# Two padding tiles made longer, so that the large tiles share one address remainder modulo 512

## Chip, cores and metric

The kernel runs on one core of one Trainium2 chip. The metric is the device time of one execution in microseconds (us); of several executions the median counts. The five engines of the core appear under their names in the profile: PE is TensorE (matrix multiply, PEld its loads of the stationary operand), DVE is VectorE, ACT is ScalarE, POOL is GpSimd and SP is SyncE, which only issues transfers here.

## What is computed

A delta-rule attention over 768 steps, then a mixture of 8 experts with Sinkhorn-normalised gates, then a gated two-matrix product with two further projections, all in float32:

```python
def _attn_ref(q, k, v, beta):            # B, H, S, D = 4, 8, 768, 48
    k_n = k / (norm(k) + 1e-6); state = zeros(B, H, D, D)
    for t in range(S):
        y[:, :, t] = einsum('bhd,bhde->bhe', q[:, :, t], state)
        v_old = einsum('bhde,bhd->bhe', state, k_n[:, :, t])
        state += beta[:, :, t] * einsum('bhd,bhe->bhde', k_n[:, :, t], v[:, :, t] - v_old)

def _moe_ref(x, w_gate, w1, w2):         # x (3072, 384), 8 experts, hidden 1024
    P = exp(x @ w_gate - max)
    for _ in range(8):
        P /= P.sum(1); P /= P.sum(0); P *= N / E
    return sum(P[:, e:e+1] * (relu(x @ w1[e]) @ w2[e]) for e in range(8))

def _moe2_ref(x, w1, w2, w3, w_out):     # (384,1024) (384,1024) (1024,1024) (1024,384)
    return (((x @ w1) * (x @ w2)) @ w3) @ w_out
```

## The kernel before

Every float32 operand of the two large products is held as two parts in the type float32r: a rounded value and the rest. A product of two operands is then three matmuls, high by high, high by low and low by high, summed in one PSUM bank. A matmul call names the output, the stationary operand (called the weights here, 128 columns, 512 bytes in each partition) and the moving operand (up to 512 columns, 2048 bytes in each partition). In the rows, `b<-hB,wA` is a matmul into a PSUM bank from operands in the tiles hB and wA; the two names stand in alphabetical order, so that they do not tell which one moves.

There are three stages.

- **Stage A** (to about 425 us): attention in 12 chunks (`prep_k`, `invert`, `tt_make`, `prep_q`, `seq`), and between them the first expert (`e0`) for the chunks that are done, with moving operands of 256 columns from xr and hA and weights from wA. The Sinkhorn loop closes the stage.
- **Stage B** (about 430 to 1745 us): experts 1 to 7. The tokens are taken in three passes of 1024, an expert in two halves, so there are 3 x 7 x 2 = 42 calls of `unit`. A unit first forms `relu(x @ w1)` from linear combinations of blocks (`product`, lines 1222 to 1228: 22 products of three matmuls, moving operands from xr and xT, weights from wA and wS), then multiplies by w2 (`m2`, lines 1270 to 1277: six groups of 12 matmuls, moving operands from hA and hB, weights from wA). All 138 matmuls of a unit have 512 columns. In the first pass the weights come from DRAM through rawB and are split on ACT and POOL; later passes load the split form (`load_pair`).
- **Stage C** (from about 1745 us): the last products, by `phase_c`. w3 and w_out are multiplied first (`m34`: moving operand wA, weights wS, 384 columns, 192 matmuls). Then come six chunks of 512 tokens. In each, 144 matmuls `ab` of 512 columns have their weights in xT and their moving operand, the tokens, in turn in wS and in xr; the 96 matmuls `om` of 384 columns have their weights in hA or hB and their moving operand in wA.

The three matmuls of one product, here in `m2`, where `hv` lies in hA or hB and `wh`, `wl` in wA:

```python
self.mm(o, wh, hv[:, 0], start=(x == 0), stop=False)
self.mm(o, wl, hv[:, 0], start=False, stop=False)
self.mm(o, wh, hv[:, 1], start=False, stop=(x == 3))
```

The order of instructions on each engine is set when the program is built, by a list scheduler (`Plan.order`) that works with cost estimates and knows nothing of addresses. The memory on the chip (SBUF, 128 partitions) is laid out by pools that `open` stacks from the left, in the order of opening, and from the right. A tile has the same address in every partition, rounded up to 32 bytes. Three tiles are never read or written, `padl`, `padr` and `padq`: they only take room and so shift what is stacked after them. `setup` opens the pools of stage A; when the preparation is done, the pool `prep` on the right is closed and rawB, sums, wS and acc are opened in its place, and later `seq` and `xst` on the left give way to xT, and hB, cv, cvr, rt, pb and tmp go to the right.

Of the kernel before, what the change touches and what calls it, by code (L numbers as in the profile page):

```python
# [7 lines left out]
F32 = mybir.dt.float32  # L8
F32R = mybir.dt.float32r
F16 = mybir.dt.float16  # L10
# [12 lines left out]
NE = 8  # L23
# [9 lines left out]
NP = 2  # L33
# [347 lines left out]
class Kernel:  # L381
# [56 lines left out]
    def setup(self):  # L438
# [2 lines left out]
        self.open("const", "left", ones=((128, 128), F32), masks=((128, 148), F32),  # L441
                  wgr=((128, 3, NE), F32), p=((128, NTT + 1, NE + 1), F32),
                  rs=((128, NTT), F32), cs=((128, NE), F32), sml=((128, 8), F32))
        self.open("wg", "left", wg=((128, 3, 2 * NE), F32R), padl=((128, 48), F32))
        self.open("wA", "left", wA=((128, EB, 1536), F32R))
        self.open("hA", "left", hA=((128, HA, 1024), F32R))
        self.open("xr", "left", xr=((128, 2, 2, 2, 3, 128), F32R))
# [7 lines left out]
        self.open("edge", "right", padr=((128, 24), F32))  # L455
        self.open("prep", "right",
                  g12=((128, NG12, 2, NG, 32), F32), a0=((128, NA0, 32, 32), F32),
                  asys=((128, 1056), F32), t=((128, 1056), F32), prod=((128, NP, 1024), F32), xs=((128, 256), F32), bq=((128, 6, 32), F32), t16=((128, 272), F32), padq=((128, 16), F32), wz=((128, 384), F16),
                  wraw=((128, 768), F32))
        self.open("dram", "left", space=DRAM, xs_d=((NCH, 2, DM, 128), F32), y0_d=((3, 128, NT), F32), p_d=((NE, NT), F32), xf_d=((4, 128, 3, 512), F32),  # L460
                  w1_d=((2, 128, 3, 1024), F32), w2_d=((2, 128, 3, 1024), F32), wo_d=((2, 128, 8, DM), F32),
# [1222 lines left out]
```

## Time and profile before

| | us |
|---|---|
| three runs, median (lowest, highest) | 2099.24 (2098.55, 2101.47) |
| the profiled execution, its own time | 2098.41 |
| its span, first to last instruction | 2096.6 |

| engine | busy us | share of the span |
|---|---|---|
| PE | 2066.3 | 99% |
| PEld | 1753.0 | 84% |
| DVE | 1227.3 | 59% |
| POOL | 794.7 | 38% |
| ACT | 729.6 | 35% |

Matmuls are pipelined: one that is recorded with 390 ns overlaps the next, and the time that a matmul takes from a row of matmuls is the distance from its start to the next start. So a PE that is busy all the time may still run through its matmuls faster or slower. That distance is not a column of the profile. It is read from the timeline, where a row gives the start of a merged group and the number of its matmuls: the start of the next group less its own start, over that number.

### The profile page before, as it was taken

The page shows a single profiled execution, that of the slowest core. Times are in us where ns is not written, and L with a number is a line of the kernel's source. Part 1 is how long each engine was busy: PE and PEld are TensorE (multiplying, and loading weights), DVE is VectorE, ACT ScalarE, POOL GpSimd, SP SyncE. Part 2 cuts the span into 40 slices and gives each one's busy share as a digit, 9 for nine tenths or more (in the row PEclk, how much of TensorE's full clock was granted, in tenths as well). Part 3 has the DMA queues.
Part 4 walks back from the last instruction along what each step waited for, and adds up shares of the span by engine and source line. Part 5 has one row for each costly group of instructions (what it writes and reads, how often), then busy time and mean ns, then how long its engine had stood idle before and what let it go on. Part 6 is the DMA issues. An engine that isn't in the chain of part 4 may idle for free.

```text
span 2096.6 us, 40059 instructions
## 1 busy us (share of the span) xinstructions
PE 2066.3 (99%) x16434; PEld 1753.0 (84%) x16434; DVE 1227.3 (59%) x1978; ACT 729.6 (35%) x1425; POOL 794.7 (38%) x866
## 2 busy tenths in 40 slices
PE   8999999999999999999999999999999999999999
PEld 7888999978888888888888888888888888988888
DVE  7989882665444445776666667766666743222222
ACT  6444443343443443422323323323323322222222
POOL 2101111067666667354454444444554544200000
PEclk9999999999999999999999999999999999999999
DMA  6333322275644545845655545755645537400000
GB/s 235 103 112 101 109 80 89 77 260 229 229 168 184 195 184 217 283 168 176 234 186 171 201 161 188 247 181 192 218 152 203 209 106 203 100 31 16 16 27 20
DMA packets 160664, 328.16 MB, mean 157 GB/s; under 512 B 14240, under 2 KB 111840, under 8 KB 148960
## 3 DMA queue, kind: packets, MB, share of 16 engines
q1 hardware_dynamic: 126592, 190.32, 26.7%
q0 software_dynamic: 33888, 135.28, 18.8%
q8 instruction: 129, 2.11, 0.4%
q14 instruction: 55, 0.45, 0.1%
HBM read 230.41 MB, written 93.95 MB: 155 GB/s over the span
## 4 chain that ended last, share of the span: by engine, by line
PE 93%; DVE 3%; DMA 2%; SPq 1%; ACT 1%; issue 1%; POOL 0%; ACTq 0%; POOLq 0%; DVEq 0%
PE b L403 93%; SPq L434 1%; DMA rawB<-in_moe_w 0%; DVE prod L414 0%; DMA xst<-xst 0%; DMA qt<-in_qT 0%; POOL sums L414 0%; DVE t L689 0%; DMA kt<-in_kT 0%; DVE acc L414 0%; DVE tt L414 0%; DMA pb<-p_d 0%; DVE cv L414 0%; ACT xst L407 0%; DMA acc<-in_moe_w 0%
## 5 line engine op out<-in xcount | busy, mean ns | idle before, releaser
L403 PE MATMUL b<-hA,wA 128*128 128x512 f32 (+1 forms) x2367 | 508.9, 354 | 0.0
L403 PEld LDWEIGHTS b<-hA,wA 128*128 128x128 f32 x2367 | 391.7, 189 | 66.4 <-DVE hA L417 0.4
L414 POOL TENSOR_TENSOR acc<-acc,tmp 128x512 f32<-128x512 f32 x252 | 334.9, 1330 | 230.8 <-DVE tmp L414 229.5
L403 PE MATMUL b<-hB,wA 128*128 128x512 f32 x1521 | 393.3, 394 | 0.0
L403 PEld LDWEIGHTS b<-hB,wA 128*128 128x128 f32 x1521 | 286.2, 188 | 65.0
L403 PE MATMUL b<-xr,wA 128*128 128x256 f32 (+1 forms) x1620 | 332.3, 339 | 4.2 <-DVE hA L417 1.0
L403 PEld LDWEIGHTS b<-xr,wA 128*128 128x128 f32 x1620 | 252.2, 191 | 41.2 <-DVE hA L417 1.7
L407 ACT ACTIVATE rt<-b 128x512 f32<-128x512 f32 x300 | 178.8, 598 | 270.2 <-PE b L403 266.0
L403 PE MATMUL b<-xT,wA 128*128 128x512 f32 x1008 | 250.6, 390 | 1.5 <-POOL wA L414 1.5
L414 DVE TENSOR_TENSOR b<-b,rt 128x512 f32<-128x512 f32 x252 | 173.3, 695 | 111.8 <-PE b L403 98.5
L403 PEld LDWEIGHTS b<-xT,wA 128*128 128x128 f32 x1008 | 189.1, 188 | 41.9 <-POOL wA L414 2.3
L403 PE MATMUL b<-xT,wS 128*128 128x512 f32 x756 | 204.4, 396 | 0.9 <-ACT rt L407 0.9
L414 POOL TENSOR_TENSOR cv<-cv 128x256 f32<-128x256 f32 (+3 forms) x175 | 128.5, 734 | 177.8 <-DVE cv L1433 96.9
L414 DVE TENSOR_TENSOR tmp<-b,pb 128x512 f32<-128x512 f32 x150 | 103.3, 689 | 141.7 <-PE b L403 136.6
L417 DVE SCALAR_TENSOR_TENSOR hA<-b,hA 128x512 fp32r<-128x512 f32 x215 | 144.4, 687 | 58.5 <-ACT hA L1238 30.1
L403 PEld LDWEIGHTS b<-xT,wS 128*128 128x128 f32 x756 | 142.4, 189 | 34.7 <-ACT rt L407 2.0
L414 DVE TENSOR_TENSOR rt<-b,rt 128x512 f32<-128x512 f32 x48 | 33.2, 691 | 189.5 <-PE b L403 189.5
L417 DVE SCALAR_TENSOR_TENSOR hB<-b,hB 128x512 fp32r<-128x512 f32 x169 | 114.2, 685 | 30.5 <-ACT hB L1238 29.9
L414 DVE TENSOR_TENSOR tmp<-b,yr 128x512 f32<-128x512 f32 x102 | 70.2, 689 | 101.5 <-PE b L403 93.3
L1238 ACT ACTIVATE hB<-b 128x512 fp32r<-128x512 f32 x169 | 100.0, 596 | 80.0 <-DVE b L414 77.7
L1238 ACT ACTIVATE hA<-b 128x512 fp32r<-128x512 f32 x167 | 97.1, 597 | 69.8 <-DVE b L414 41.8
L414 POOL TENSOR_TENSOR wA<-rawB,wA 128x768 fp32r<-128x768 f32 (+1 forms) x49 | 88.3, 1811 | 84.0 <-ACT wA L407 83.8
(204 smaller groups left out, 2378.7 us busy)
## 6 DMA issues: line engine op xcount, KB each, us to landing
wA<-wq_d POOLq DMA_DIRECT2D x56, 1536.0 KB, 8.9
wq_d<-wA SPq DMA_DIRECT2D x28, 1536.0 KB, 7.0
wS<-ws_d POOLq DMA_DIRECT2D x56, 512.0 KB, 4.7
rawB<-in_moe_w SPq DMA_DIRECT2D x108, 192.0 KB, 3.2
ws_d<-wS SPq DMA_DIRECT2D x28, 512.0 KB, 6.0
w_d<-cv SPq DMA_DIRECT2D x112, 128.0 KB, 1.8
cvr<-in_w3T SPq DMA_DIRECT2D x32, 256.0 KB, 2.6
wS<-w_d POOLq DMA_DIRECT2D x32, 256.0 KB, 3.4
```

What stands on the lines that cost most here:

```text
L403: self.nc.tensor.matmul(*args, skip_group_check=True, **kw)
L407: self.nc.scalar.activation(out=out, in_=in_, func=AF.Copy, **({} if scale is None else {"scale": scale}))
L414: self.E[eng].tensor_tensor(out=out, in0=in0, in1=in1, op=op)
L417: self.nc.vector.scalar_tensor_tensor(out=out, in0=in0, scalar=scalar, in1=in1, op0=op0, op1=op1)
L434: return self.g.op({eng: cost}, lambda _: e.dma_start(out=out(), in_=in_()), r=r, w=w, prio=prio, nbytes=nbytes, lat=lat)
L1238: g.op({"ACT": actb(512)}, lambda e: nc.scalar.activation(out=hv(0), in_=self.ps(s, 512), func=AF.Relu), r=[s], w=[(out, 0, 0)], prio=pe)
```

## The change

```diff
-        self.open("wg", "left", wg=((128, 3, 2 * NE), F32R), padl=((128, 48), F32))
+        self.open("wg", "left", wg=((128, 3, 2 * NE), F32R), padl=((128, 80), F32))
...
-                  ... t16=((128, 272), F32), padq=((128, 16), F32), wz=((128, 384), F16),
+                  ... t16=((128, 272), F32), padq=((128, 112), F32), wz=((128, 384), F16),
```

`padl` grows by 32 numbers, 128 bytes in each partition, and every tile on the left from wA on moves up by 128 bytes. `padq` grows by 96 numbers, 384 bytes, and the tiles of `prep` that stand ahead of it move down by 384. No instruction is added, removed, reordered or reshaped on any engine; the two programs differ in SBUF addresses alone. The addresses, in bytes within a partition:

| tiles | before | remainder mod 512 | after | remainder |
|---|---|---|---|---|
| wA | 19200 | 256 | 19328 | 384 |
| hA | 68352 | 256 | 68480 | 384 |
| xr | 84736 | 256 | 84864 | 384 |
| yr | 97024 | 256 | 97152 | 384 |
| xT (stages B, C); kraw (stage A) | 100096 | 256 | 100224 | 384 |
| kn, kt, qt, pt, tt, vs, st, u (stage A) | 109312 to 171776 | 256 | each 128 higher | 384 |
| xst (stage A) | 179840 | 128 | 179968 | 256 |
| g12, a0, asys (stage A) | 189440, 197632, 205824 | 0 | each 384 lower | 128 |
| prod (stage A) | 214272 | 256 | 213888 | 384 |
| hB | 170880 | 384 | the same | 384 |
| wS | 203648 | 384 | the same | 384 |
| rt, pb, tmp, cv, cvr, acc, rawB | 149376 to 220032 | 384 | the same | 384 |

Within these tiles the operands of the matmuls of stages B and C begin at multiples of 512 bytes, so that the remainder of a tile is that of each of its operands there. Because 384 down and 128 up are the same modulo 512, the tiles of stage A in the lists above keep their remainders relative to each other.

## Rows read from the trace of the kernel before

**Rows 1.** The page: the span, and busy time of each engine with its instructions
```profile
span 2096.6 us, 40059 instructions
...
PE 2066.3 (99%) x16434; PEld 1753.0 (84%) x16434; DVE 1227.3 (59%) x1978; ACT 729.6 (35%) x1425; POOL 794.7 (38%) x866
```

**Rows 2.** The chain that ended last, in order of time: start us, length us, what
```profile
430.73 475.74 PE b L403 x2061
...
910.87 438.43 PE b L403 x1902
...
1356.87 736.20 PE b L403 x3378
```

**Rows 3.** Stretches of stage B: length, busy PE, PEld, DVE, ACT, POOL, clock, DMA
```profile
440.00:900.00 460.00, 460.00 (x1995) 374.67 (x1994) 240.66 (x359) 176.97 (x319) 295.66 (x308) 1.00 0.56 206
920.00:1340.00 420.00, 420.00 (x1825) 342.91 (x1824) 288.72 (x479) 137.42 (x264) 192.73 (x218) 1.00 0.57 195
1360.00:1740.00 380.00, 380.00 (x1651) 310.27 (x1650) 242.47 (x399) 120.20 (x226) 180.15 (x196) 1.00 0.54 185
```

**Rows 4.** Timeline of PE in stage C: start us, length us, what
```profile
1884.83 4.39 PE L403 MATMUL b<-wA,hB 128*128 128x384 f32 x24
1889.06 4.34 PE L403 MATMUL b<-wA,hA 128*128 128x384 f32 x24
1893.24 32.84 PE L403 MATMUL b<-xr,xT 128*128 128x512 f32 x144
1925.92 2.27 PE L403 MATMUL b<-wA,hA 128*128 128x384 f32 x12
...
1942.78 33.76 PE L403 MATMUL b<-wS,xT 128*128 128x512 f32 x144
1976.37 4.33 PE L403 MATMUL b<-wA,hA 128*128 128x384 f32 x24
```

**Rows 5.** Timeline of PE in stage B, the end of one unit's products and what follows
```profile
722.70 2.88 PE L403 MATMUL b<-xT,wA 128*128 128x512 f32 x12
725.42 0.86 PE L403 MATMUL b<-hB,wA 128*128 128x512 f32 x3
...
727.23 2.25 PE L403 MATMUL b<-hB,wA 128*128 128x512 f32 x9
729.32 0.86 PE L403 MATMUL b<-hA,wA 128*128 128x512 f32 x3
```

**Rows 6.** Groups by line and shape, PE: operands, count, busy us, mean ns, idle before
```profile
L403 PE MATMUL b<-hB,wA 128*128 128x512 f32 x1521 | 393.3, 394 | 0.0
...
L403 PE MATMUL b<-hA,wA 128*128 128x512 f32 x1503 | 386.1, 392 | 0.0
...
L403 PE MATMUL b<-xT,wS 128*128 128x512 f32 x756 | 204.4, 396 | 0.9 <-ACT rt L407 0.9
...
L403 PE MATMUL b<-wS,xT 128*128 128x512 f32 x432 | 101.1, 395 | 0.0
...
L403 PE MATMUL b<-xr,xT 128*128 128x512 f32 x432 | 99.9, 390 | 0.0
...
L403 PE MATMUL b<-xr,wS 128*128 128x512 f32 x252 | 65.9, 395 | 0.3 <-ACT rt L407 0.3
...
L403 PE MATMUL b<-wA,hB 128*128 128x384 f32 x324 | 59.2, 338 | 0.0
```

**Rows 7.** What PE waited for, 430 to 2097 us: total us, times, longest us
```profile
PE b L403 <- ACT rt L407: 1.2, 3, 0.7
```

**Rows 8.** Timeline of PE in stage A, a run of warming matmuls on wz alone
```profile
54.76 1.92 PE L403 MATMUL b<-wz 128*128 128x256 f16 x16
```

**Rows 9.** Instructions on the tile wz: shortest, median, longest ns, first and last start
```profile
L403 PE MATMUL b<-wz x161: 272/273/422, 15.2 to 57.9; 128*128 128x256 f16 x161
```

**Rows 10.** What PE waited for, whole span: the longest in total
```profile
PE b L403 <- DMA kt<-in_kT: 9.0, 3, 4.2
```

**Rows 11.** DMA issues: count, KB each, median us from issue to landing
```profile
wA<-wq_d POOLq DMA_DIRECT2D x56, 1536.0 KB, 8.9
```

More of the change, by code (lines that the diff above doesn't have):

```diff
@@ L457, in setup @@
                   g12=((128, NG12, 2, NG, 32), F32), a0=((128, NA0, 32, 32), F32),
-                  asys=((128, 1056), F32), t=((128, 1056), F32), prod=((128, NP, 1024), F32), xs=((128, 256), F32), bq=((128, 6, 32), F32), t16=((128, 272), F32), padq=((128, 16), F32), wz=((128, 384), F16),
+                  asys=((128, 1056), F32), t=((128, 1056), F32), prod=((128, NP, 1024), F32), xs=((128, 256), F32), bq=((128, 6, 32), F32), t16=((128, 272), F32), padq=((128, 112), F32), wz=((128, 384), F16),
                   wraw=((128, 768), F32))
```

## The prediction

> **What bounds the kernel now.** I read the page first: PE is busy in 99% of the span [rows 1]. Then the chain of work that ended last. From 430 us to the end it is almost nothing but matmuls on PE, in three pieces of 475.7, 438.4 and 736.2 us [rows 2], and in the whole of that time PE waited only 1.2 us for others [rows 7]. So stages B and C last as long as PE needs to run through its matmuls, and the question is how far their starts lie apart. The stretches give it: in stage B 1995 matmuls start in 460 us, 1825 in 420 and 1651 in 380 [rows 3], together 5471 in 1260 us, 230.3 ns each. [...]
>
> Are these 230 ns the same for every matmul? The timeline of stage C holds a natural experiment. Two chunks run the same 144 matmuls with the same weights in xT; only the tokens lie in xr in the one and in wS in the other. With xr the next group starts 1925.92 - 1893.24 = 32.68 us later, 226.9 ns a matmul; with wS it is 1976.37 - 1942.78 = 33.59 us, 233.3 ns [rows 4]. PE waits for nothing in either. Before the change xr and xT both leave 256 when divided by 512, while wS leaves 384. The same shows in stage B: 12 matmuls on xT and wA (256 and 256) take 725.42 - 722.70 = 2.72 us, 226.7 ns each, and a little later 9 on hB and wA (384 and 256) take 729.32 - 727.23 = 2.09 us, 232.2 ns each [rows 5]. The groups by shape say it for all: pairs with unequal remainders are recorded with 394 to 396 ns, the equal pair xr, xT with 390 [rows 6]. The records overlap, so only the difference counts there.
>
> One row looks like a contradiction: hA and wA have equal remainders and yet 392 ns [rows 6]. My reading is that a matmul's cost hangs on its own moving operand and on the weights that are being loaded for the next one, and that a delay of that kind needs several matmuls to die away. In stage B groups of both kinds alternate every 3 to 12 matmuls, so an equal pair often still carries what its unequal predecessors left. The 12 on xT and wA stand behind other equal pairs and are clean.
>
> **The change part by part.** No instruction, wait or transfer is added or moved; only addresses change. Afterwards wA, hA, xr and xT leave 384, as hB and wS already do. Every operand pair of stages B and C is then an equal pair, and there are no changes of kind left.
>
> Stage B: 42 units x 138 = 5796 matmuls of 512 columns. They take 230.3 ns [rows 3] and would take 226.7 [rows 5]: 3.6 x 5796 = 20.9 us less. With 226.9 [rows 4] for the clean value it is 19.7.
>
> Stage C, 512 columns: three of the six chunks have their tokens in wS (432 matmuls, rows 6), each 33.59 - 32.68 = 0.91 us longer than a chunk on xr [rows 4]: 2.7 us less.
>
> Stage C, 384 columns: 24 matmuls with weights in hB take 1889.06 - 1884.83 = 4.23 us, 176.3 ns each, and 24 with weights in hA 1893.24 - 1889.06 = 4.18 us, 174.2 ns [rows 4]. For the 324 with hB [rows 6] and the 192 of `m34` with wS, which has the same remainder, that is 2.1 ns x 516 = 1.1 us less.
>
> Stage A: nothing. Its moving operands xr and hA and the weights wA have equal remainders now and after, and the attention tiles all move by the same amount modulo 512. A shift of both operands that changed something after all would show in stages B and C first; that is the slower rival below.
>
> What PE gives back: in a unit of 31.8 us the others get 0.5 us less time. PE waits 1.2 us now, in three waits for a copy to rt on ACT [rows 7], which is where the chain breaks between its pieces [rows 2]. Where PE waits already, it waits up to 0.5 us longer; with a few more such places I take 1 us. The bounds are 0 and, if every one of 42 units were at its limit, 21 us; the lower end is far nearer, since DVE, the busiest helper, works 289 of 420 us [rows 3] and nearly all units have no wait. Weights for a unit are loaded during the one before, 8.9 us from issue to landing [rows 11] in 31, so their cover stays.
>
> [...]
>
> Sum: 20.9 + 2.7 + 1.1 = 24.7, less 1, is 23.7 us. The profiled execution took 2098.4 us (its span is 2096.6), so it would take 2074.7. The median of the runs lies 0.8 above the profiled one: 2075.5.
>
> **The rivals.** *Only part of it goes.* If the 392 ns of hA, wA [rows 6] are that pair's own price and no after-effect, equal remainders alone do not bring 226.7. The unequal pairs then fall to about the level of hA, wA: 1521 on hB, wA by 2 ns, 756 on xT, wS by 4 and 252 on xr, wS by 3, which is 3.0 + 3.0 + 0.8 us, and stage C gives its 3.8. That is 10.6 us, and less the 1 of new waits the time comes near 2089.6. Against it speaks that the same xT, wA is clean when it stands behind equal pairs.
>
> *Slower: what matters is the multiple of 256.* In the fast pairs of before both operands start at a multiple of 256; in the slow ones one of them starts 128 past it. No pair of stages B and C has both there, and after the change all have. If a start off that multiple is the price, every matmul pays the 233.3 ns of the wS chunk: 3.0 x 5796 = 17.4 us more in stage B, 3 x 0.91 = 2.7 in the chunks on xr, and 2.1 ns for each of the 252 of 384 columns with hA (576 `om` less 324 with hB [rows 6]), 0.5; 20.6 us, so 2098.4 + 20.6 + 0.8 = 2119.8. If each operand pays for itself it is more. It decides from the first pair that has both operands off, which is every pair after the change. Against it: the warming matmuls have weights and moving operand in wz, both 128 past a multiple of 256, and 16 of them take 1.92 us [rows 8]; less the last one's own length of 0.27 [rows 9] that is 1.65 us over 15 starts, 110 ns for 256 columns, no sign of a stall. But these are 16-bit numbers, half the bytes, and their remainders (128 and 384) differ.
>
> *No change.* What sets xr apart from wS could be something that the change leaves as it is, such as their distance in memory. Then 233.3 and 226.9 ns both stay and the time is 2099.2. [...] Against this rival speaks too that four kinds of unequal pairs, wherever their tiles lie, are recorded with 394 to 396 ns and the equal one on xr, xT with 390 [rows 6].
>
> **How the numbers follow.** The forecast 0.70, the part 0.11, no change 0.07, slower 0.12. The predicted time is the first one's, 2075.5. Its own bounds are 2073 (a clean value of 226.4 and no wait given back) and 2080 (226.9 and 4 us of new waits). The range goes on to the partial case, to 2091, and leaves out no change and slower, 0.19. At the low end I go to 2069, since no pair at 384 and 384 has been seen and it could be cleaner still. A measurement of this kernel tells about 0.2%, 4 us, from no change. Faster by more: 0.70 + 0.11 = 0.81; within: 0.07; slower by more: 0.12.
>
> **What would show it.** In the changed kernel's timeline the chunks on wS should take 32.7 us as those on xr do, 9 matmuls on hB and wA 2.04 us, and the groups by shape should show 389 to 390 ns for every 512-column pair, hA with wA too. Stretches of stage B should hold 4.41 matmuls a microsecond instead of 4.34. If hA, wA stays at 392 among equal pairs, the after-effect was misread. If all pairs rise to 394 or more, the multiple of 256 is what counts. If PE's waits in stage B grow from 1.2 us to more than 5, the other engines are later than I think.

## The result

The changed kernel takes 2075.62 us (median of four runs, 2074.32 to 2079.69), the kernel before, beside it on the same chip, 2100.35 (2098.55 to 2102.31). The ratio is 0.9885, with a 95% interval of 0.9868 to 0.9902: 1.2% faster. The forecast was 2075.5. The profiled execution took 2075.69 us, 22.7 less than that of before. Timed again on another chip, the changed kernel took 2077.91 us, a ratio of 0.9898 (0.9883 to 0.9913).

The page of the changed kernel, as [rows 1]: PE is still busy nearly all the time, and the other engines do the same work in the same time. Only PE's own busy time is shorter.

```profile
span 2073.9 us, 40059 instructions
...
PE 2040.9 (98%) x16434; PEld 1747.7 (84%) x16434; DVE 1227.6 (59%) x1978; ACT 730.2 (35%) x1425; POOL 795.4 (38%) x866
```

The stretches of stage B in the changed kernel (length, then busy time and instructions of PE, PEld, DVE, ACT, POOL, clock, DMA), as [rows 3]:

```profile
440.00:900.00 460.00, 459.18 (x2023) 379.05 (x2022) 245.98 (x365) 177.81 (x321) 299.71 (x311) 1.00 0.57 207
920.00:1330.00 410.00, 410.00 (x1808) 339.00 (x1808) 284.76 (x475) 137.80 (x265) 191.25 (x217) 1.00 0.57 198
1345.00:1720.00 375.00, 375.00 (x1656) 310.51 (x1655) 242.53 (x401) 121.01 (x228) 179.94 (x196) 1.00 0.55 190
```

5487 matmuls start in 1245 us, one every 226.9 ns, where it was 230.3. That is 4.41 a microsecond, at the same granted clock of 1.00.

PE's timeline in stage C of the changed kernel (start us, length us, what), as [rows 4]:

```profile
1872.73 32.84 PE L403 MATMUL b<-xr,xT 128*128 128x512 f32 x144
1905.41 2.27 PE L403 MATMUL b<-wA,hA 128*128 128x384 f32 x12
1907.52 4.32 PE L403 MATMUL b<-wA,hB 128*128 128x384 f32 x24
1911.67 2.24 PE L403 MATMUL b<-wA,hA 128*128 128x384 f32 x12
...
1922.07 32.84 PE L403 MATMUL b<-wS,xT 128*128 128x512 f32 x144
1954.76 4.35 PE L403 MATMUL b<-wA,hA 128*128 128x384 f32 x24
```

The chunk on xr takes 1905.41 - 1872.73 = 32.68 us as before, and the chunk on wS now takes 1954.76 - 1922.07 = 32.69 us instead of 33.59. The 24 matmuls of 384 columns with weights in hB take 4.15 us, 172.9 ns each, instead of 176.3.

The groups by shape of the changed kernel (operands, count, busy us, mean ns, idle before), as [rows 6]: every pair with 512 columns is now at one level, 389 to 390 ns.

```profile
L403 PE MATMUL b<-hB,wA 128*128 128x512 f32 x1521 | 386.4, 389 | 0.0
L403 PE MATMUL b<-hA,wA 128*128 128x512 f32 x1503 | 382.2, 389 | 0.5 <-ACT hA L1238 0.5
...
L403 PE MATMUL b<-xr,wA 128*128 128x512 f32 x756 | 205.5, 389 | 0.0
L403 PE MATMUL b<-xT,wS 128*128 128x512 f32 x756 | 199.2, 390 | 1.2 <-ACT rt L407 1.2
L403 PE MATMUL b<-xr,xT 128*128 128x512 f32 x432 | 100.0, 390 | 0.0
L403 PE MATMUL b<-wS,xT 128*128 128x512 f32 x432 | 98.5, 389 | 0.0
L403 PE MATMUL b<-xr,wS 128*128 128x512 f32 x252 | 64.5, 390 | 1.3 <-ACT rt L407 1.3
L403 PE MATMUL b<-wA,hB 128*128 128x384 f32 x324 | 58.3, 334 | 0.0
```

What PE waited for in the changed kernel from 425 us on (total us, times, longest us), as [rows 7]:

```profile
PE b L403 <- ACT rt L407: 2.5, 4, 1.0
PE b L403 <- ACT hA L1238: 0.5, 1, 0.5
```

And its chain of waits, as [rows 2] (start us, length us, what), which now breaks once more, at that wait for hA at 723 us:

```profile
463.17 241.71 PE b L403 x1065
723.06 177.39 PE b L403 x780
...
904.95 431.84 PE b L403 x1902
...
1344.37 725.92 PE b L403 x3378
```

The last two pieces hold the same 1902 and 3378 matmuls as before and are 6.6 and 10.3 us shorter.

### The profile page after: what moved, and what is told of

It reads as the page before. It is cut to its first block, busy times and chain, and to the rows that moved or that the text cites. A ratio compares the mean times of both kernels' runs of the same rounds, so it can differ in the third digit from the quotient of the medians.

```text
span 2073.9 us, 40059 instructions
## 1 busy us (share of the span) xinstructions
PE 2040.9 (98%) x16434; PEld 1747.7 (84%) x16434; DVE 1227.6 (59%) x1978; ACT 730.2 (35%) x1425; POOL 795.4 (38%) x866
## 4 chain that ended last, share of the span: by engine, by line
PE 88%; issue 4%; DMA 2%; DVE 2%; ACT 1%; POOL 1%; SPq 1%; POOLq 0%; ACTq 0%; DVEq 0%
PE b L403 88%; SPq L434 1%; POOL wA L414 1%; DMA yr<-in_moe_w 1%; DMA rawB<-in_moe_w 0%; DMA vs<-in_v 0%; DMA kt<-in_kT 0%; DMA xst<-xst 0%; POOL acc L414 0%; DVE t L689 0%; DVE prod L414 0%; DVE asys L723 0%; DVE a L725 0%; POOL sums L414 0%; DVE cv L414 0%
## 5 line engine op out<-in xcount | busy, mean ns | idle before, releaser
L403 PE MATMUL b<-hB,wA 128*128 128x512 f32 x1521 | 386.4, 389 | 0.0
L414 DVE TENSOR_TENSOR b<-b,rt 128x512 f32<-128x512 f32 x252 | 172.9, 695 | 103.2 <-ACT rt L407 72.2
L403 PE MATMUL b<-xT,wS 128*128 128x512 f32 x756 | 199.2, 390 | 1.2 <-ACT rt L407 1.2
```

The source lines that it names most:

```text
L403: self.nc.tensor.matmul(*args, skip_group_check=True, **kw)
L414: self.E[eng].tensor_tensor(out=out, in0=in0, in1=in1, op=op)
```

## The experiments

All kernels compute the whole reference. They differ from the kernel before in the length of tiles that are never read. The left tiles (wA, hA, xr, xT) move with `padl`; hB and wS move together with `padr`, and e5_hB_only has one more such tile, `padh`; `padq` keeps the remainders of stage A's other tiles relative to the left ones. In the table the remainders are modulo 512. The last column is taken from each profiled execution and leaves out stage A and the first few matmuls of stage B: the end of the span less the start of the first group of 12 matmuls on xT and wA in stage B (it starts at 436.36 us before and at 436.68 in the changed kernel). The ratio is to the kernel before on the same chip.

| kernel | left | hB | wS | median us (lowest, highest) | ratio (95%) | stages B, C |
|---|---|---|---|---|---|---|
| before | 256 | 384 | 384 | 2100.35 (2098.55, 2102.31) | 1 | 1660.2 |
| changed | 384 | 384 | 384 | 2075.62 (2074.32, 2079.69) | 0.9885 (0.9868, 0.9902) | 1637.2 |
| e12_changed_again | 384 | 384 | 384 | 2077.91 (2077.42, 2079.5) | 0.9898 (0.9883, 0.9913) | 1636.4 |
| e7_padl_only | 384 | 384 | 384 | 2073.73 (2071.86, 2078.47) | 0.9879 (0.9865, 0.9893) | 1636.1 |
| e8_padq_only | 256 | 384 | 384 | 2098.14 (2096.6, 2110.85) | 1.0003 (0.9987, 1.0019) | 1660.1 |
| e1_all256 | 256 | 256 | 256 | 2074.91 (2073.8, 2078.87) | 0.9882 (0.9868, 0.9897) | 1636.8 |
| e6_all352 | 352 | 352 | 352 | 2076.44 (2075.34, 2077.17) | 0.9886 (0.9871, 0.9901) | 1637.1 |
| e5_hB_only | 256 | 256 | 384 | 2087.39 (2085.32, 2094.57) | 0.9945 (0.9928, 0.9963) | 1648.1 |
| e2_diff256 | 128 | 384 | 384 | 2078.77 (2072.53, 2081.86) | 0.9894 (0.9874, 0.9913) | 1636.1 |
| e4_diff32 | 352 | 384 | 384 | 2103.21 (2098.25, 2105.05) | 1.0008 (0.9987, 1.0028) | 1662.2 |
| e3_diff64 | 320 | 384 | 384 | 2104.9 (2100.97, 2108.18) | 1.002 (1.0009, 1.0031) | 1663.1 |
| e11_diff96 | 288 | 384 | 384 | 2105.09 (2100.44, 2108.66) | 1.0015 (0.9999, 1.0031) | 1662.5 |
| e10_diff192 | 192 | 384 | 384 | 2096.02 (2094.26, 2098.87) | 0.9979 (0.9965, 0.9992) | 1655.8 |

The last column falls into two levels, 1636 to 1637 us and 1656 to 1663, with e5_hB_only half way. The rest of the scatter lies in stage A, whose length differs by 2.6 us between the two profiled executions of the changed kernel alone.

### Which of the two tiles does it

```diff
e7_padl_only
-  padl=((128, 48), F32)
+  padl=((128, 80), F32)
e8_padq_only
-  padq=((128, 16), F32)
+  padq=((128, 112), F32)
```

> One part of the change alone: padl longer, padq as before. The tiles of stages B and C stand exactly as in the changed kernel; in stage A the prep tiles (g12, a0, asys, prod) keep their old remainders and so stand 128 bytes apart from the left tiles as compared with before. If the gain is all in stages B and C: 2075.6 us, the same as the whole change. If the remainders between prep tiles and left tiles matter in stage A, it is slower than the whole change by what stage A then takes longer, at most some us.

> The other part alone: padq longer, padl as before. Stages B and C stand as before the change, hB, wA at 394 ns; the prep tiles of stage A are moved by 128 modulo 512 against the left tiles. Expected 2099 to 2101 us, no change, unless stage A feels it; then the first matmul of stage B starts later than at about 424 us.

`padl` alone gives 0.9879, all of the gain; `padq` alone 1.0003, nothing. So the gain belongs to the four left tiles, and the attention tiles of stage A, whose distance to the left ones `padq` keeps, have no part in it that these runs can tell.

### Is it the equality, or where the operands start

```diff
e1_all256
-  padr=((128, 24), F32)        padq=((128, 16), F32)
+  padr=((128, 56), F32)        padq=((128, 112), F32)
e6_all352
-  padl=((128, 48), F32)        padr=((128, 24), F32)        padq=((128, 16), F32)
+  padl=((128, 72), F32)        padr=((128, 32), F32)        padq=((128, 112), F32)
```

> All large tiles at remainder 256 instead of 384: the left side as before the change, the right side moved down by 128 bytes; the prep tiles keep their remainders relative to the left. If only the difference of the two operands' remainders counts, this is the changed kernel again: about 2075.6 us, every 512-column pair recorded with 389 to 390 ns, chunks on wS in stage C 32.7 us. If a start at a multiple of 256 were better in itself than one 128 past it, it would be faster than the changed kernel; if remainder 384 itself were what helps, it would stay near 2100.

> All large tiles at remainder 352, an odd multiple of 32 bytes, left and right alike. If only the difference counts: 2075.6 us within 0.2%, 389 to 390 ns for every 512-column pair. If starts at multiples of 64, 128 or 256 matter as such: slower, with 394 ns or more for all pairs and a total of 2100 or more; transfers that start at odd multiples of 32 could also make stage A some us longer.

All at 256 gives 0.9882 and all at 352 gives 0.9886, the changed kernel (all at 384) 0.9885. PE's timeline of e1_all256 shows the wS chunk clean too, 1953.65 - 1920.97 = 32.68 us:

```profile
1920.97 32.84 PE L403 MATMUL b<-wS,xT 128*128 128x512 f32 x144
1953.65 4.35 PE L403 MATMUL b<-wA,hA 128*128 128x384 f32 x24
```

So with the same remainder on both sides it makes no difference in these three kernels where the operands start, at 256, at 384 or, with 352, at an odd multiple of 32 bytes. That shows the rival with the multiples of 256 to be wrong from two sides: 384 is as good as 256, and so is 352.

### Remainders that differ by 256

```diff
e2_diff256
-  padl=((128, 48), F32)        padq=((128, 16), F32)
+  padl=((128, 16), F32)        padq=((128, 48), F32)
```

> Left tiles at remainder 128, right tiles at 384: the difference is 256. If the period is 512 as the change takes it, unequal pairs cost as much as with a difference of 128 or more: hB, wA 394 ns, wS chunks 33.3 to 33.6 us, total 2095 to 2105 us. If the period is 256, this is as good as the changed kernel: 2075.6 us, 389 ns, 32.7 us.

Here the left tiles leave 128 and the right ones 384: unequal modulo 512, equal modulo 256. PE's timeline in stage C of this kernel:

```profile
1925.96 32.84 PE L403 MATMUL b<-wS,xT 128*128 128x512 f32 x144
1958.64 4.35 PE L403 MATMUL b<-wA,hA 128*128 128x384 f32 x24
```

Again 32.68 us, and stages B and C take 1636.1 us, so a difference of 256 costs no more here than equal remainders do (32.69 and 1637.2 us in the changed kernel). The condition in the change's description, equal modulo 512, is therefore stronger than it had to be. No other difference of 256 was run.

### The after-effect

```diff
e5_hB_only
-  self.open("hBp", "right", hB=((128, HB, 1024), F32R))
+  self.open("hBp", "right", hB=((128, HB, 1024), F32R), padh=((128, 32), F32))
```

> The kernel before, with hB alone (and the tiles cv, cvr, rt, pb, tmp, which PE never reads) moved down by 128 bytes to remainder 256; wS stays at 384. So hB, wA becomes an equal pair, while xT, wS and xr, wS in stage B and wS, xT in stage C stay unequal. After-effect theory: the hA, wA pair, whose own addresses are untouched, falls from 392 to 389 or 390 ns, because nothing unequal stands near it any more, while xT, wS stays at 395 or 396; total near 2088 us (of the 24.7 us of change, 1521 matmuls on hB at 4 to 5 ns and the after-effect on hA). Rival, hA, wA has a price of its own: it stays at 392 ns and the total is near 2093.

This brings hB to 256, beside wA and hA at 256, and leaves wS at 384. The tiles cv, cvr, rt, pb and tmp, which PE never reads, move with hB; nothing is altered about hA and wA. The groups by shape of this kernel:

```profile
L403 PE MATMUL b<-hB,wA 128*128 128x512 f32 x1521 | 386.3, 389 | 0.0
L403 PE MATMUL b<-hA,wA 128*128 128x512 f32 x1503 | 381.7, 389 | 0.0
...
L403 PE MATMUL b<-xr,wA 128*128 128x512 f32 x756 | 208.3, 393 | 0.0
L403 PE MATMUL b<-xT,wS 128*128 128x512 f32 x756 | 204.4, 396 | 1.0 <-ACT rt L407 1.0
```

hA, wA falls from 392 [rows 6] to 389 ns with its own addresses untouched, because its neighbours on hB have become equal pairs. xr, wA, an equal pair as well, stays at 393 between the unequal groups on wS. So the 392 of before was no price of the pair itself. How long the after-effect lasts stands in the trace of before: in groups of nine on hA, wA between groups on hB the distances from start to start are 228, 236, 228, 232 and 231 ns on average, and then four times 227. The time of 2087.39 us is about half way: w2's products are clean, those that read wS are not.

### How the cost depends on the difference

```diff
e4_diff32
-  padl=((128, 48), F32)        padq=((128, 16), F32)
+  padl=((128, 72), F32)        padq=((128, 120), F32)
e3_diff64
+  padl=((128, 64), F32)        padq=((128, 128), F32)
e11_diff96
+  padl=((128, 56), F32)        padq=((128, 136), F32)
e10_diff192
+  padl=((128, 32), F32)        padq=((128, 32), F32)
```

> Left tiles at remainder 352, right at 384: the two sides differ by 32 bytes. All or nothing: wS chunks 33.6 us, total near 2100. In proportion: a quarter, wS chunks 32.9 us, total near 2081. If the two streams share lines of 64 bytes or more, nothing: 32.7 us and 2076.

> Left tiles at remainder 320, right at 384: the two sides differ by 64 bytes. What is known: differences of 0 and 256 give 226.7 ns a matmul, 128 gives 233.3 in the chunks on wS (33.6 us). All or nothing: any difference that is no multiple of 256 costs the same, so the wS chunks take 33.6 us and the total is near 2100. In proportion to the distance from a multiple of 256: about half, wS chunks 33.1 us, total near 2088.

> Left tiles at remainder 288, right at 384: the difference is 96, the nearest to 128 that the layout allows. All or nothing: wS chunks 33.6 us, total near 2100, as with 128. In proportion: three quarters, wS chunks 33.4 us, total near 2094.

> Left tiles at remainder 192, right at 384: the difference is 192, which is 64 short of 256. If only the difference modulo 256 counts and its sign does not, this equals the run with a difference of 64; all or nothing would put the wS chunks at 33.6 us and the total near 2100.

In the wS chunks, matmuls of 512 columns, the cost does not grow with the difference: 32 bytes cost as much as 96 or 128. The chunk takes 33.60 us in e4_diff32 (1944.41 to 1978.01), in e11_diff96 (1950.77 to 1984.37) and in e10_diff192, where it was 33.59 with 128 [rows 4]. The timeline of e10_diff192 reads:

```profile
1940.45 33.76 PE L403 MATMUL b<-wS,xT 128*128 128x512 f32 x144
1974.05 4.33 PE L403 MATMUL b<-wA,hA 128*128 128x384 f32 x24
```

With 64 it is not so. PE's timeline in stage C of e3_diff64, where the weights in xT lie 64 below the moving operand in wS (modulo 256):

```profile
1952.70 33.13 PE L403 MATMUL b<-wS,xT 128*128 128x512 f32 x144
1985.66 4.35 PE L403 MATMUL b<-wA,hA 128*128 128x384 f32 x24
```

That is 32.96 us, 228.9 ns a matmul, a third of the usual cost. In e10_diff192 the products that take weights from wS have the same relation, since 192 above is 64 below modulo 256. They too are cheap there, as its timeline in stage B shows beside that of e3_diff64, where the sign is the other one. e10_diff192:

```profile
713.99 1.54 PE L403 MATMUL b<-xT,wS 128*128 128x512 f32 x6
715.36 0.84 PE L403 MATMUL b<-xr,wA 128*128 128x512 f32 x3
```

e3_diff64:

```profile
719.84 1.56 PE L403 MATMUL b<-xT,wS 128*128 128x512 f32 x6
721.24 0.86 PE L403 MATMUL b<-xr,wA 128*128 128x512 f32 x3
```

Six matmuls take 1.37 us (228.3 ns each) in the first and 1.40 (233.3) in the second. Over all matmuls on xT, wS, without the gaps at waits, the distances are 229.2 and 233.5 ns. This is the main reason why e10_diff192 is the only one of the four that is faster than before: some 4 ns on 1008 matmuls are 4 us, and its stages B and C are 4.4 us shorter. Two other changes nearly cancel: xr, wA behind these groups falls from 230.2 to 226.8 ns, 2.5 us less, and hB, wA rises from 231.6 to 233.3, 2.6 us more. But hB, wA does not fit. In e3_diff64 these weights also lie 64 below the moving operand, and yet they stay dear:

```profile
L403 PE MATMUL b<-hB,wA 128*128 128x512 f32 x1521 | 395.0, 395 | 0.0
...
L403 PE MATMUL b<-hA,wA 128*128 128x512 f32 x1503 | 389.8, 394 | 0.0
```

So "64 below is cheap" held for three of four kinds of pairs (wS, xT; xT, wS; xr, wS) and not for the fourth. What sets that one apart was not found.

The matmuls of 384 columns follow another pattern, which the total hides because they are few. In them the weights in hB and wS lie above the moving operand in wA. A row of e4_diff32 in stage C:

```profile
1982.19 4.33 PE L403 MATMUL b<-wA,hB 128*128 128x384 f32 x24
1986.36 2.27 PE L403 MATMUL b<-wA,hA 128*128 128x384 f32 x12
```

The 24 take 4.17 us, 173.8 ns each, where it was 176.3 with a difference of 128 [rows 4]. Over all matmuls on hB of this kind, differences of 32, 96 and 192 give 173.5 to 173.8 ns, as good as the 173.6 of the changed kernel; 128 gives 176.1 and 64 gives 176.5. `m34`, with weights in wS, goes the same way (173.6 to 173.8 ns at 32, 96 and 192, 176.3 at 128, 175.5 at 64, 174.4 in the changed kernel). So an unequal pair is not dear in every shape: at 384 columns 32, 96 and 192 bytes cost nothing that these numbers show.

In e2_diff256, e3_diff64 and e11_diff96 stage A of the profiled execution is 5.4 to 6.1 us longer than before. One profile each does not tell whether the addresses do that (more on it below, under stage A); it is no part of the last column.

### The changed kernel beside them

> The changed kernel once more, beside its two parts on the same chip: 2075.6 us, ratio to the kernel before 0.9885.

It was run once more with e7_padl_only and e8_padq_only on their chip. 2077.91 us against the 2073.73 of e7_padl_only is 0.2%, and stages B and C differ by 0.3 us: the difference is stage A's, 439.31 against 434.05 us to the same group, and more than the 2.6 us between two executions of one kernel. Whether `padq` costs a little there stays open.

## Why the prediction was right

**What bounds the kernel.** Right. With the same instructions, the same clock and nearly the same waits, a shorter distance between starts on PE came through to the end almost whole: of about 25 us that PE runs faster, 22.7 are in the span. Stages B and C take 1637.2 instead of 1660.2 us, 23.0 less, where the sum said 23.7. That the median came within 0.1 us of the forecast is luck: the profiled execution took 2075.69 us, 1.0 more than the 2074.7 of the sum, and the median of the changed kernel lies 0.1 below its profiled execution where the prediction added 0.8. Single runs of it differ by 5 us.

**Stage B.** Foreseen were 226.7 ns instead of 230.3. The stretches show 226.9 with the new waits in them, which by 5796 matmuls is 19.7 us rather than 20.9; without the gaps at waits the groups in the timeline start every 226.7 ns for hB, wA and hA, wA alike. Nine matmuls on hB and wA were to take 2.04 us, and in the changed kernel's timeline they do, 728.91 - 726.87:

```profile
726.87 2.20 PE L403 MATMUL b<-hB,wA 128*128 128x512 f32 x9
728.91 0.84 PE L403 MATMUL b<-hA,wA 128*128 128x512 f32 x3
```

The reading that the prediction needed most, the 392 ns of hA, wA as an after-effect of its neighbours, is shown by e5_hB_only. The rival in which only part of the gain comes rested on the opposite and falls with it. The kernel before had a second row of the kind, which the prediction passed over:

```profile
L403 PE MATMUL b<-xr,wA 128*128 128x512 f32 x756 | 208.3, 393 | 0.0
```

This equal pair too is at 389 ns in the changed kernel.

**Stage C.** 0.8 to 0.9 us for each of three wS chunks, 2.6 us, where 2.7 was foreseen. The 384-column matmuls with hB gained 3.4 ns in the rows above rather than 2.1, and 2.5 ns over all of them, too little to matter.

**The new waits.** Here a term came out too small in this pair of profiles. 1 us was foreseen; the waits named in the profile grew from 1.2 to 3.0 us, and all gaps between starts from the beginning of stage B (424 us) on that go beyond the normal distance, added up over the trace, from 2.8 to 5.3 us. That is 2.5 us given back, at the same few places where one pass of tokens ends or the first unit begins, at one for hA near 723 us, which grew from 0.4 to 1.1 us, and at a new one near 1254 us. In the other two profiles with these tiles in stages B and C the gaps add up to 4.3 (e12_changed_again) and 3.7 us (e7_padl_only), so 1 to 2.5 us are given back from one execution to the next. In almost all of the 42 units the helpers were early enough, as their busy shares let expect.

**Stage A.** Nothing was foreseen, and the first groups of stage B start within 0.4 us of before. In the changed kernel PE waits 10.2 us for kt, whose remainder is now 384, instead of 9.0 [rows 10]:

```profile
PE b L403 <- DMA kt<-in_kT: 10.2, 4, 4.2
```

One pair of profiles tells little here: the other two profiles with kt at 384 (e12_changed_again, e7_padl_only) have 12.1 and 9.2 us. All thirteen together lean to longer waits where kt does not start at 256, without showing it. The four with kt at 256 wait 8.5 to 10.5 us, 9.5 on average; the nine with kt elsewhere wait 9.2 to 12.6, 11.1 on average, and the groups at the start of stage B come 434.7 to 437.6 us into the span in the four (436.1 on average) and 434.1 to 442.5 in the nine (438.7). In the total e1_all256, which starts its transfers at 256 and has equal pairs, is no faster than the changed kernel within the intervals. So a price of one to three us is possible, it is an eighth of the gain at most, and it stays open.

**Slower, by the multiples of 256.** Wrong: e1_all256 and e6_all352 tell it apart from the equality, and both agree with the equality.

**No change.** The distance in memory that the change leaves as it is (some 119,000 bytes between xr and wS) is not it: 128 bytes decide (e7_padl_only, 0.9879). The same 144 matmuls take 32.68 us in e1_all256 and e2_diff256 and 33.60 in e4_diff32 and e11_diff96, by the remainders of their two operands alone.

**What stays open.** Whether the moving operand collides with its own weights or with the weights that are being loaded for the next matmul (in the trace of before that load starts 3 ns after the matmul, in the median, and is 188 ns long). In all pairs of these runs both come from the same tile, apart from the edges of groups, and the edges tell a part. At 39 places of stage B the last of six or more matmuls on xT and wA, an equal pair, is followed by one on xT and wS. In the kernel before the next start comes 232.7 ns after that last one (231 to 234), and 226.6 ns after those ahead of it; in the changed kernel it is 226.6 for all. So the delay comes already before the first matmul with unequal weights starts, in the stretch in which the trace has these weights loaded. At other differences the timelines give whole groups: 15 matmuls on xT and wA ahead of such an edge, 3.400 us in the changed kernel and 3.407 before, take on average 3.400 in e10_diff192 (192), 3.402 in e11_diff96 (96), 3.403 in e3_diff64 (64) and 3.408 in e4_diff32 (32). The matmuls on xT and wS behind them start every 229.2, 233.3, 233.5 and 233.0 ns, so the one does not foretell the other. Whether a matmul's own weights cost as well cannot be told there from the after-effect. No run shows what it is in the engine or the memory that collides, if it is a collision. And it stays open why 64 below is cheap in three kinds of pairs and dear in the fourth, and why 32 and 96 cost nothing at 384 columns.

## What to carry to other kernels

Where PE runs matmul after matmul without a wait, look at the distance from start to start for each pair of operands, in long runs in the timeline. Here the busy share (99% before, 98% after) hid a difference of 3% between pairs (226.7 against 233.3 ns), and in the recorded durations (389 against 394 to 396 ns) it looked like half of that. If pairs differ, try the weights and the moving operand at the same remainder modulo 256 (here it was worth 23 to 25 us of 2100, and an unused tile of 128 more bytes brought it). A pair that looks like an exception may only stand behind bad neighbours: repair these and look again before giving it a price of its own.

## What the runs showed of the hardware that was not expected

- Remainders of 128 and 384 go together without cost, where 256 and 384 do not: 32.68 us for a wS chunk in e2_diff256, 33.59 before. The one difference of 256 that was run is as good as none.
- With 512 columns, in the wS chunks, a difference of 32, 96 or 128 bytes costs the same 0.9 us in 33.6 (e4_diff32, e11_diff96, before), and one of 64 a third of it (32.96 us, e3_diff64). With 384 columns and the weights above the moving operand, 32 and 96 cost nothing (173.5 to 173.8 ns against 173.6) and 128 costs 2.5 ns (176.1).
- A difference of 64 has a sign: 228.9 to 229.2 ns with the weights 64 below the moving operand (modulo 256; e3_diff64 in stage C, e10_diff192 in stage B), 233.3 to 233.5 with them 64 above, against 226.7 for equal remainders; hB, wA is the exception with 232.4 at 64 below (e3_diff64).
